# Narrower v pieces between the scores, weighted values in pairs, a first layer begun on two head pairs, two pieces swapped and one copy moved to ScalarE

## The chip, the cores and the metric

The kernel runs on one core of one Trainium2 chip. The metric is the time of one execution on the device, in microseconds (us). Each kernel was executed several times, in rounds in which the kernel before ran beside it on the same chip. Every execution counted here was fast (none was over 1.5% above the fastest of its kernel). Within that state the clock granted to TensorE (the share of its full rate that the profile shows as allowed) still differed from launch to launch (its mean over an execution was 0.968 to 0.978 in all runs but four, and 0.961 to 0.963 in those).

## The reference, cut to what matters

Attention over blocks of 96 tokens, with k and v mixed between blocks by a matrix P that five row and column normalisations make, then two dense layers with a squared Relu between.

```python
# q, k, v: 4 x 8 heads x 768 x 64; 8 blocks of 96 tokens; P: 4 x 8 x 8 x 8
k_sorted = np.einsum('bhij,bhjcd->bhicd', P, k_b)
v_sorted = np.einsum('bhij,bhjcd->bhicd', P, v_b)
...
attn = softmax(scale * q_b @ k_sb.T)      # inside each block
x    = (attn @ v_sb)                      # 3072 tokens x 512
h = x @ w_in                              # 512 x 2048
g = s * np.maximum(h, 0.0)**2 + b
out = g @ w_out                           # 2048 x 512
```

## The kernel before

Tokens are worked on in eight groups `t` of 384 (half of one batch's sequence). What concerns us is the start: the first group's attention, which has nothing else to run beside, and the first layer (`ffn1`) that follows it. Later groups' attention is cut into pieces that a queue puts between the matmuls of the layers.

```python
def warm_up(n, pool=psb):                 # dummy matmuls: 128 rows, 256 columns
    wp = pool.tile([128, 256], FP, ...)
    for _ in range(n):
        nc.tensor.matmul(out=wp, lhsT=zt[:, 0:128], rhs=zt, start=True, stop=True)

def v_piece0(d0, n, eng):                 # n of the 64 columns of sorted v
    # n > 8: a buffer of pool psa (3 of them); n <= 8: one of pool psb (2)
    ...                                   # n matmuls, one eviction on eng

def ffn1(t, slot=nothing, n0=0, nn=HB):   # first layer, 8 groups of 2 x 128 features
    for f0 in range(0, NF, 2):
        hps = psa.tile([128, 2, 512], FP, tag="a", name="hps")
        for f in range(2):
            for hp in range(NHP):         # 4 head pairs: 8 matmuls to a group
                nc.tensor.matmul(out=hps[:, f, 0:nt], lhsT=wi_at(hp, f0 + f), ...)
        rt = rtp.tile(...)
        nc.scalar.activation(out=rt, in_=hps, func=AF.Relu)          # ACT
        nc.vector.tensor_tensor(out=gt[...], in0=rt, in1=rt, op=ALU.mult)  # DVE
        slot()                            # a piece of other work
...
v_piece0(0, 16, "v")
v_piece0(16, 16, "s")
v_piece0(32, 16, "v")
s_piece(0, 0)                             # scores of a head pair, Exp on ACT
v_piece0(48, 8, "v")
s_piece(0, 1)
v_piece0(56, 8, "v")
s_piece(0, 2)
s_piece(0, 3)
for hp in range(NHP):
    p_piece(0, hp, 0, 2)                  # weighted values: 4 matmuls, then x on DVE
    if hp == 3:
        t_part(0, 0, "s", 0, 2)           # transposes of x, copy on ACT
    warm_up(2, psa)                       # two dummies after each: 8 here
t_part(0, 2, "v", 0, 2)
warm_up(2, psa)                           # and two more: 10 in all
```

In the profile, `tv` is a v piece, `sc` scores, `pv` weighted values, `x` their normalised form, `tr` transposes, `hps` the first layer, `rt` its Relu, `gt` the square, `ops` the second layer, `wp` a dummy. A dummy is a matmul whose result nobody reads; it is there to keep PE at work.

The softmax here doesn't subtract the row's maximum and nothing guards it: scores larger than these inputs give would overflow.

## Time and profile before

| what | value | where from |
|---|---|---|
| time | 233.06 us (233.01 to 233.14, 3 runs) | times |
| span of the profiled execution | 231.6 us | page |
| PE busy | 224.3 us, 97% | page, part 1 |
| DVE, ACT busy | 116.8 and 114.6 us, about 50% each | page, part 1 |
| clock at half rate | from 14.11 to 27.77 us | granted clock, read in ever narrower windows |
| first layer starts | 27.32 us | timeline |

PE, busy for 97% of the span, is the engine that bounds the kernel, so time leaves the total only where PE waits or runs at half clock.

### The profile page before, as it was taken

The numbers are of one execution on the slowest core, as the hardware profiler recorded it, in microseconds if no ns is written. First come the engines' busy times: TensorE is split into PE (matmuls) and PEld (weight loads), VectorE is DVE, ScalarE is ACT, GpSimd is POOL, SyncE is SP. The second block draws the span as 40 slices with busy tenths as digits, with TensorE's granted clock in tenths as the row PEclk, the third lists the DMA queues.
The fourth block names the chain that finished last, engine by engine and source line by source line (L and its number), as shares of the span: only waits on it lengthen the run. The fifth ranks groups of instructions, "written<-read, shape, count | busy, mean of one in ns | idle before, by whom it ended". The sixth has DMA issues, their size and how long they took to land.

```text
span 231.6 us, 4837 instructions
## 1 busy us (share of the span) xinstructions
PE 224.3 (97%) x2036; PEld 136.8 (59%) x2036; DVE 116.8 (50%) x245; ACT 114.6 (49%) x164; POOL 48.3 (21%) x62
## 2 busy tenths in 40 slices
PE   8879999999999999999999999999999999999994
PEld 6779887765544555566555555665555556554442
DVE  5778566638992645244446653343452634432221
ACT  6168479685158486856630645656222236660000
POOL 7820000399992000007920000000000000000000
PEclk9975699999999999999999999999999999999999
DMA  5999999998799992764999995610115240001212
GB/s 93 142 200 211 226 193 205 231 220 183 106 110 180 273 312 63 161 82 65 130 148 133 183 197 115 93 47 0 46 47 113 93 110 4 3 0 45 80 59 91
DMA packets 46695, 28.90 MB, mean 125 GB/s; under 512 B 35921, under 2 KB 41041, under 8 KB 46161
## 3 DMA queue, kind: packets, MB, share of 16 engines
q0 software_dynamic: 18800, 15.21, 47.8%
q1 hardware_dynamic: 27728, 13.32, 26.6%
q8 instruction: 16, 0.26, 0.5%
q10 hardware_dynamic: 144, 0.07, 0.1%
q14 instruction: 7, 0.05, 0.1%
HBM read 29.63 MB, written 8.65 MB: 165 GB/s over the span
## 4 chain that ended last, share of the span: by engine, by line
PE 82%; DVE 7%; DMA 5%; ACT 3%; issue 1%; POOL 0%; POOLq 0%
PE hps L473 35%; PE ops L516 31%; DMA qr<-in_q_dram 5%; PE pv L402 4%; PE sc L375 3%; DVE gt L478 2%; ACT ks L240 2%; DVE ks L238 2%; PE tv L320 2%; PE ops L501 2%; PE tk L294 1%; PE tv L350 1%; PE wp L182 1%; PE tq L254 1%; PE tv L336 1%
## 5 line engine op out<-in xcount | busy, mean ns | idle before, releaser
L473 PE MATMUL hps<-xt,wi 128*128 128x384 bf16 (+1 forms) x576 | 87.1, 309 | 0.3 <-ACT rt L477 0.3
L516 PE MATMUL ops<-wo,gt 128*128 128x512 bf16 x368 | 86.9, 380 | 0.4 <-DVE ot L490 0.4
L473 PEld LDWEIGHTS <-wi 128*128 128x128 bf16 x576 | 54.1, 98 | 30.6 <-issue 1.3
L477 ACT ACTIVATE rt<-hps 128x768 bf16<-128x768 f32 (+1 forms) x72 | 53.1, 741 | 37.4 <-PE hps L473 37.0
L478 DVE TENSOR_TENSOR gt<-rt 128x768 bf16<-128x768 bf16 (+1 forms) x72 | 41.2, 574 | 50.2 <-ACT rt L477 50.0
L516 PEld LDWEIGHTS <-gt 128*128 128x128 bf16 x368 | 33.6, 98 | 37.2 <-issue 1.0
L378 ACT ACTIVATE at<-sc 96x768 bf16<-96x768 f32 x32 | 24.4, 804 | 27.7 <-PE sc L375 27.7
L490 DVE SCALAR_TENSOR_TENSOR ot<-ops,s_bc,bias 128x512 f32<-128x512 f32 x23 | 17.1, 749 | 41.2 <-PE ops L516 41.2
L240 ACT CAST ks<-tk 64x512 bf16<-64x512 f32 (+1 forms) x32 | 18.6, 582 | 10.5 <-PE tk L294 10.2
L407 DVE TENSOR_TENSOR x<-pv,rec 96x512 bf16<-96x512 f32 (+1 forms) x36 | 22.6, 627 | 1.3
L639 POOL TENSOR_TENSOR csum<-csum,wo 128x512 f32<-128x512 f32 x14 | 17.6, 1254 | 1.0
L402 PEld LDWEIGHTS <-at 96*128 96x128 bf16 (+1 forms) x256 | 12.0, 104 | 3.8
L182 PE MATMUL wp<-zt 128*128 128x256 bf16 x86 | 12.9, 311 | 1.1 <-DVE warm L113 1.1
L238 DVE CAST ks<-tk 64x512 bf16<-64x512 f32 (+1 forms) x20 | 13.0, 651 | 1.1 <-PE tk L294 0.8
L402 PE MATMUL pv<-vs,at 96*128 96x66 bf16 (+1 forms) x256 | 13.0, 199 | 0.1
L240 ACT CAST vn<-tv 128x512 bf16<-128x512 f32 (+1 forms) x12 | 9.4, 799 | 7.2 <-PE tv L350 5.0
L375 PEld LDWEIGHTS <-ks 64*96 64x96 bf16 x256 | 8.6, 128 | 5.8 <-issue 5.1
L406 DVE RECIPROCAL rec<-pv 96x8 f32<-96x8 f32 (+1 forms) x36 | 6.9, 192 | 9.5 <-PE pv L402 9.4
L84 POOL DMA_DIRECT2D qr<-in_q_dram x12 | 10.6, 912 | 4.8 <-DMA kb<-in_k_dram 3.1
L375 PE MATMUL sc<-qt,ks 64*96 64x96 bf16 x256 | 10.9, 219 | 0.1
L182 PEld LDWEIGHTS <-zt 128*128 128x128 bf16 x86 | 9.0, 110 | 2.6 <-DVE warm L113 1.1
L294 PEld LDWEIGHTS <-kb 64*128 64x128 bf16 x192 | 6.7, 99 | 3.9 <-issue 3.4
(73 smaller groups left out, 98.4 us busy)
## 6 DMA issues: line engine op xcount, KB each, us to landing
out_dram<-ot SPq DMA_DIRECT2D x23, 256.0 KB, 2.4
kb<-in_k_dram POOLq DMA_DIRECT2D x4, 768.0 KB, 12.2
vb<-in_v_dram POOLq DMA_DIRECT2D x4, 768.0 KB, 19.0
wi<-in_moe_w_in_dram POOLq DMA_DIRECT2D x2, 1024.0 KB, 19.7
wo<-in_moe_w_out_dram POOLq DMA_DIRECT2D x2, 1024.0 KB, 32.6
qr<-in_q_dram POOLq DMA_DIRECT2D x12, 128.0 KB, 13.5
dv<-vn SPq DMA_DIRECT2D x6, 256.0 KB, 7.5
vs<-dv POOLq DMA_DIRECT2D x4, 384.0 KB, 12.7
```

The source lines that it names most:

```text
L182: nc.tensor.matmul(out=wp, lhsT=zt[:, 0:128], rhs=zt, start=True, stop=True)
L238: nc.vector.tensor_copy(out=out, in_=in_)
L240: nc.scalar.copy(out=out, in_=in_)
L375: nc.tensor.matmul(out=sc[:, e, n * BLK:(n + 1) * BLK], lhsT=ks[pr, g0 + n, :], rhs=QT[b][pr, hp, q0:q0 + BLK], start=True, stop=True)
L378: nc.scalar.activation(out=at, in_=sc[:, :, 0:TG], func=AF.Exp, scale=scale)
L402: nc.tensor.matmul(out=pv[e][0:m, (n - n0) * VW:(n - n0 + 1) * VW], lhsT=atf[:, c0:c0 + m], rhs=VS[b][:, gi, :], start=True, stop=True)
L407: nc.vector.tensor_tensor(out=x[:, n0:n0 + nn, hp * 128:(hp + 1) * 128].rearrange("p n (e d) -> p e n d", e=2), in0=pvv[:, :, :, 0:D], in1 ...
L473: nc.tensor.matmul(out=hps[:, f, 0:nt], lhsT=wi_at(hp, f0 + f), rhs=xt_at(t, hp, n0, nn), start=(hp == 0), stop=(hp == NHP - 1))
L477: nc.scalar.activation(out=rt[:, :, 0:nt], in_=hps[:, :, 0:nt], func=AF.Relu)
L478: nc.vector.tensor_tensor(out=gt[:, f0:f0 + 2, c0:c0 + nt], in0=rt[:, :, 0:nt], in1=rt[:, :, 0:nt], op=ALU.mult)
L516: nc.tensor.matmul(out=ops, lhsT=gt[:, f, m * 128:(m + 1) * 128], rhs=wo_at(f), start=(f == 0), stop=(f == NF - 1))
L639: nc.gpsimd.tensor_tensor(out=csum, in0=csum, in1=wo_at(f), op=ALU.add)
```

## The change

Its intent: in the stage ahead of the first layer, put a score piece after every 8-wide v piece, make two head pairs' weighted values share one buffer and one DVE product, and let the first layer begin two groups on the head pairs whose transposed x arrives first. Further on, it swaps a v piece with a weighted-values piece, and moves one copy of transposed q from DVE to ScalarE. I call these part 1, part 2 and part 3.

```diff
+    def p_pair(t, hp0, n0):                        # 8 matmuls, one buffer
+        p2 = psa.tile([128, 4, 256], FP, tag="a", name="pv")
...                                                 # one reciprocal, one product on DVE
-    def ffn1(t, slot=nothing, n0=0, nn=HB):
+    def ffn1(t, slot=nothing, n0=0, nn=HB, lead=0):
...
+        for f0 in range(0, lead, 2):
+            begun[f0] = psa.tile([128, 2, 512], FP, tag="a", name="hps")
+            products(f0, begun[f0], range(0, NHP // 2))
...
-    v_piece0(32, 16, "v")
-    s_piece(0, 0)
-    v_piece0(48, 8, "v")
-    s_piece(0, 1)
-    v_piece0(56, 8, "v")
-    s_piece(0, 2)
-    s_piece(0, 3)
     for hp in range(NHP):
-        p_piece(0, hp, 0, 2)
-        if hp == 3:
-            t_part(0, 0, "s", 0, 2)
-        warm_up(2, psa)
+        v_piece0(32 + 8 * hp, 8, "v")
+        s_piece(0, hp)
+    warm_up(2)
+    p_pair(0, 0, 0)
+    warm_up(2)
+    p_pair(0, 2, 0)
+    t_part(0, 0, "s", 0, 2)
+    warm_up(3)
     t_part(0, 2, "v", 0, 2)
-    warm_up(2, psa)
...
-                   ... SC(1, 0), SC(1, 1)], 8), 0, 2)
-    ffn1(0, Queue([..., V1(1), P(1, 2), P(1, 3),
+                   ... SC(1, 0), SC(1, 1)], 8), 0, 2, 4)
+    ffn1(0, Queue([..., P(1, 2), V1(1), P(1, 3),
...
-    qu = Queue([nothing, lambda: q_piece(1, 2, "v")]
+    qu = Queue([nothing, lambda: q_piece(1, 2, "s")]
```

More of the change, by code (lines that the diff above doesn't have):

```diff
@@ L410, in p_piece @@
             in1=rec[:, :, 0:nn].unsqueeze(3).broadcast_to([BLK, 2, nn, D]), op=ALU.mult)
+    def p_pair(t, hp0, n0):
+        b, half = divmod(t, 2)
+        if t not in X:
+            X[t] = xp.tile([BLK, HB, d_model], BF, tag="x", name="x")
+        p2 = psa.tile([128, 4, 256], FP, tag="a", name="pv")
+        for i in range(2):
+            atf = AT[t, hp0 + i].rearrange("p e t -> p (e t)")
+            for e in range(2):
+                for n in range(2):
+                    c0 = (e * HB + n0 + n) * BLK
+                    gi = e * 32 + (hp0 + i) * NB + half * HB + n0 + n
+                    nc.tensor.matmul(out=p2[:, 2 * i + e, n * VW:(n + 1) * VW],
+                                     lhsT=atf[:, c0:c0 + 128], rhs=VS[b][:, gi, :],
+                                     start=True, stop=True)
+        pvv = p2[0:BLK, :, 0:2 * VW].rearrange("p a (n w) -> p a n w", w=VW)
+        rec = rtp.tile([BLK, 4, 2], FP, tag="rec", name="rec2")
+        nc.vector.reciprocal(out=rec, in_=pvv[:, :, :, D])
+        nc.vector.tensor_tensor(
+            out=X[t][:, n0:n0 + 2, hp0 * 128:(hp0 + 2) * 128].rearrange(
+                "p n (a d) -> p a n d", d=D),
+            in0=pvv[:, :, :, 0:D], in1=rec.unsqueeze(3).broadcast_to([BLK, 4, 2, D]),
+            op=ALU.mult)
     def t_piece(t, eng, n0=0, nn=HB):
@@ L468, in ffn1, with products @@
         c0, nt = n0 * BLK, nn * BLK
-        for f0 in range(0, NF, 2):
-            hps = psa.tile([128, 2, 512], FP, tag="a", name="hps")
+        begun = {}
+        def products(f0, hps, part):
             for f in range(2):
-                for hp in range(NHP):
+                for hp in part:
                     nc.tensor.matmul(out=hps[:, f, 0:nt], lhsT=wi_at(hp, f0 + f),
@@ L475, in ffn1 @@
                                      start=(hp == 0), stop=(hp == NHP - 1))
+        for f0 in range(0, lead, 2):
+            begun[f0] = psa.tile([128, 2, 512], FP, tag="a", name="hps")
+            products(f0, begun[f0], range(0, NHP // 2))
+        for f0 in range(0, NF, 2):
+            if f0 in begun:
+                hps = begun[f0]
+                products(f0, hps, range(NHP // 2, NHP))
+            else:
+                hps = psa.tile([128, 2, 512], FP, tag="a", name="hps")
+                products(f0, hps, range(NHP))
             rt = rtp.tile([128, 2, TG], BF, tag="rt", name="rt")
@@ L621 @@
     ffn1(0, Queue([P(0, 0, 2, 2), P(0, 1, 2, 2), P(0, 2, 2, 2), P(0, 3, 2, 2),
-                   lambda: q_half(1, "s"), lambda: t_piece(0, "v", 2, 2), SC(1, 0), SC(1, 1)], 8), 0, 2)
-    ffn1(0, Queue([seq(SC(1, 2), P(1, 0)), V1(0), seq(SC(1, 3), P(1, 1)), V1(1), P(1, 2), P(1, 3),
+                   lambda: q_half(1, "s"), lambda: t_piece(0, "v", 2, 2), SC(1, 0), SC(1, 1)], 8), 0, 2, 4)
+    ffn1(0, Queue([seq(SC(1, 2), P(1, 0)), V1(0), seq(SC(1, 3), P(1, 1)), P(1, 2), V1(1), P(1, 3),
                    seq(V1(2), V1(3)), lambda: t_piece(1, "v")], 8), 2, 2)
```

## The prediction

> **What bounds the kernel now.** I read the page first, then the busy time and granted clock by window, then the timeline and the chain of waits in the three places that the change touches.
>
> ```profile
> PE   8879999999999999999999999999999999999994
> PEclk9975699999999999999999999999999999999999
> ...
> PE 82%; DVE 7%; DMA 5%; ACT 3%; issue 1%; POOL 0%; POOLq 0%
> ```
> TensorE is busy nearly everywhere and is 82% of the chain that ended last. From about 70 us on the chain lists almost only PE pieces, so a microsecond taken out before that should come out of the total. But slices 2 to 4 ran at a reduced clock. The windows[...]:
>
> ```profile
> 17.52:20.93 3.41, 3.27 (x41) 3.22 (x41) 2.60 (x4) 3.10 (x6) 0.00 (x0) 0.50 1.13 211
> 20.93:24.35 3.42, 3.32 (x55) 3.14 (x54) 2.69 (x5) 2.63 (x4) 0.53 (x1) 0.50 1.12 213
> 24.35:27.75 3.40, 3.40 (x32) 2.76 (x31) 2.56 (x8) 0.97 (x2) 0.00 (x0) 0.50 1.16 226
> 27.75:31.17 3.42, 3.42 (x51) 3.22 (x50) 2.15 (x9) 1.75 (x4) 0.00 (x0) 1.00 1.03 198
> ```
> Columns: busy PE, weight loads, DVE, ACT, POOL, then the clock. The clock is 0.50 until 27.75 us, so the stage that the change rebuilds (v pieces, scores, first weighted values, 16.2 to 27.3 us) runs wholly at half rate. PE is covered, yet two dependences matter there:
>
> ```profile
> 14.86 4.80 ACT L240 CAST ks<-tk 64x512 bf16<-64x512 f32 x8
> ...
> 22.97 0.69 DVE L238 CAST vs<-tv 96x512 bf16<-96x512 f32 x1 [0.20 <-PE tv L320]
> ...
> 27.32 1.05 PE L473 MATMUL hps<-xt,wi 128*128 128x192 bf16 x8
> ```
> ACT's eight key evictions end at 19.66. The last v eviction (22.97 to 23.66) releases the first weighted values. The first layer starts at 27.32. Later, in the chain of waits:
>
> ```profile
> 41.75 0.68 PE hps L473 x8
> 42.42 0.02 issue
> 42.45 0.50 ACT rt L477
> 42.95 0.04 issue
> 42.99 0.82 PE hps L473 x8
> ```
> PE waits for a Relu that frees a PSUM buffer, about 0.47 us.
>
> ```profile
> 57.19 4.29 DVE gt L478 x3
> 61.48 1.67 DVE qt L238
> 63.15 0.59 DVE ks L238
> ...
> 68.73 0.76 DVE bias L561
> 69.52 0.76 DVE ot L490
> 70.28 0.04 issue
> 70.32 1.02 PE ops L516 x4
> ```
> DVE is a chain without a gap from 57 to 70.3 us, and PE waits at its end.
>
> [...] half rate lasts from 14.11 to 27.75 us, four times 3.41. So time saved before 27.75 is worth half[...]. [...] the 128x768 squares take 557 ns at 49.4 us and 1507 ns by 57.1 us, while GpSimd sums w_out; this is why DVE is late, and the change leaves it alone.
>
> **Part 1: the stage to the first layer.** The same 64 v and 32 score matmuls remain; the v pieces become 16, 16, 8, 8, 8, 8, with a score piece after each 8. I took each wait from the order of instructions and the semaphores of the changed program, and each duration from the trace.
> - Before, the third v piece (16) takes a buffer that is free and starts at 19.36 without a wait. After, the first 8-piece takes the small buffer whose ACT evictions end at 19.66: start 19.71, a new wait of 0.35.
> - At half rate an 8-piece costs 0.70 and a score piece 0.31 (8 v plus 8 scores: 21.07 to 22.08). Four pairs from 19.71 end at 23.73 (before: 23.37).
> - The last 8-piece ends on PE about 23.6 (23.43 plus its latency); its DVE eviction (0.69) ends at 24.33 (before 23.66). The two dummy matmuls fit in the gap. First pair of weighted values: 24.38 to 24.83 on PE, results 25.03.
> - DVE per pair: reciprocal 0.20 + product 0.69 = 0.92 with the issue, against 2 x 0.65 = 1.30 for two single ones (0.18 + 0.42 and gaps). First pair's x at 25.98; second pair's results at 25.94, x at 26.92.
> - First transposes 26.04 to 26.36; three dummies (0.21 each) to 27.0; second transposes 27.0 to 27.32. ACT's copy of the first half is done at 27.12. So the first layer starts at 27.32, by chance the same as before.
> - Beginning two groups on head pairs 0 and 1 puts 8 matmuls ahead of the copy on DVE (done 27.99). Before, two dummies (0.42) did that. Dummies go from 10 to 7, but the time goes into the wait for v and into DVE.
> Sum: 0.0, give or take 0.3, since what is gained or lost runs at half rate. A gain beyond 0.38 would meet the second half of w_in, which landed at 30.42 and is first read at 30.80.
>
> **Part 2: value piece swapped.** Now: group 3 of the second half at 39.56, v piece 40.31, group 4 40.64, values 41.31, group 5 41.58, values 42.25, group 6 42.99. The last step takes 0.74 where the same step earlier takes 0.27: 0.47 of wait. Changed: group 3 39.56, values 40.23, group 4 ready at 40.50 but its buffer is freed by the DVE product that ends at 40.74, so 40.79 (new wait 0.28); v piece 41.54, group 5 41.87, values 42.54, group 6 42.81; its buffer was free by 42.13. Gain 0.47 - 0.28 = 0.18.
>
> **Part 3: q copy on ScalarE.** ACT is idle from 58.97 to 63.75. ACT took 1.44 for the same copy at 47.19; from 60.65 it ends at 62.1, before ACT's next piece at 63.75: free. DVE loses 1.67. The key matmuls of 61.54 release their results at 62.18, so DVE then does four evictions of 0.69 to 65.0, four more to 68.07 (results there from 65.26), bias to 68.85 (was 69.48), output row to 69.64 (was 70.27). PE: from the start of the scores at 69.18 to the next w_out group took 1.13 us; the same step at 72.57 took 0.49. The excess, 0.64, is two waits: the second score piece for bias (0.14 or more) and the group for the row. Afterwards the group could start at 69.67 and is released at 69.69. Gain 0.62.
>
> Total: 0.0 - 0.18 - 0.62 = -0.80 us, all ahead of the PE-bound stretch: 233.06 - 0.80 = 232.26.
>
> **Rivals.**
> - The clock comes back one window later (31.17), because three dummies are gone and PE waits 0.3 for x: then 3.41 us at half rate cost about 1.7, giving 234.0. For: window 24.35 to 27.75 falls from 3.40 busy to about 3.0 (estimate from the starts above). Against: the first rise, three windows before 14.11 at 3.87, followed a window in which PE had worked only from 1.13 on, 2.74 of 3.41, with the same dummies. About 8%.
> - It comes back one window earlier, at 24.35, because scores are packed with v: about 0.6 better, 231.6. Against: that window keeps about the same matmuls and had not sufficed. About 5%.
> - Part 1 gains what its author hoped: if the 0.35 wait or the late v eviction is hidden better than I think, 0.2 to 0.3 more, 232.0.
> - The gain is absorbed: GpSimd's sum of w_out ends at 64.96 whatever PE does (its start follows the last x at 44.3); the bias matmul needs it, at 66.06 before. The slack of 1.1 holds against 0.2 of shift. Value reads of batch 1 landed at 71.07 and are needed at 76.3. If DVE stays late anyway (squares slower still), part 3 gives only part of 0.62: 232.6.
>
> **Range and chances.** Parts 2 and 3 rest on waits measured to some 0.1; part 1 is worth 0.3 either way; the clock adds a tail on both sides. Range 231.7 to 233.1. No route reaches 2% (4.7 us): even a clock two windows off is less. Faster 0.01, same 0.98, slower 0.01.
>
> **What would show it.** Right: half rate still ends at 27.75; the first 8-wide v piece starts at 19.7, after ACT; the first layer starts near 27.3; no Relu wait of 0.5 near 42.5 but a DVE wait of 0.3 near 40.6; no PE wait for the output row near 70, and the w_out group that began at 70.32 begins about 69.5. Wrong: a first layer start off by more than 0.3, a clock record moved by a window, or PE still waiting for DVE at 69 to 70 us.

The sum: 0.0 - 0.18 - 0.62 = -0.80 us, that is 232.26 us. To read with it:

- A "window" there and below is a stretch of 3.41 us, counted from a change of the clock. The measure comes from these profiles: full rate held for 10.24 us (3 x 3.41) from 3.87 to 14.11 us, half rate for 13.65 (4 x 3.41) to 27.77. The rise at 3.87 shows in the dummies, which start 0.21 us apart before it and 0.11 after (the clock column has no record from before 3.87 and prints 1.00 there). What the two rivals on the clock give as reasons (dummies, waits, packing) were conjectures when they were written.
- "Worth half" is an estimate from the granted clock of 0.50 up to 27.75. The pair's times on DVE (0.20 and 0.69) are estimates from the same shapes later in this trace: a reciprocal of 96x8 took 197 ns and a product of 96x512 took 686 ns on average. The "latency" is 0.2 us: the last v piece starts at 22.08, its matmuls account for 0.70, and its eviction starts at 22.97.
- GpSimd's sums of w_out run from 44.73 to 64.96 us, beside the short square and the long ones alike. That they are what slows the squares was not shown.

## The result, and the profile after

The changed kernel took 233.84 us (median of 4 runs, 233.58 to 233.99). The kernel before took 233.10 us in the same rounds (4 runs, 233.01 to 233.14). The ratio is 1.0031, with a 95% interval from 1.0014 to 1.0049. Ratios here and below are the mean time of one kernel's fast runs over the mean of the other's in the same rounds, so they are not quite the ratio of the medians quoted. In these rounds the change made the kernel a little slower. I had expected 0.80 us less, and 233.1 at the most.

The two profiles, by their landmarks (us from the start of the span):

| landmark | before | after | after minus before |
|---|---|---|---|
| first weighted values on PE | 23.71 | 24.41 | +0.70 |
| first layer starts | 27.32 | 27.31 | -0.01 |
| clock is full again | 27.77 | 29.48 | +1.71 |
| q transposes inside the first layer | 31.60 | 32.67 | +1.07 |
| first layer of t=1 starts | 47.08 | 48.10 | +1.02 |
| w_out group after the bias | 70.32 | 70.75 | +0.43 |
| span | 231.6 | 232.2 | +0.6 |

The stage itself came out as worked out. The whole loss arises between the first layer's start and the q transposes, some 5 us; part 2 gives back 0.05 and part 3 gives back 0.59.

The page of the changed kernel, with busy PE and the granted clock:

```profile
PE   8979999999999999999999999999999999999994
PEclk9985599999999999999999999999999999999998
```

Each digit is a fortieth of the span (5.8 us). PE is filled as before. The clock row is different: the reduced slices have moved to the right.

The windows of the changed kernel, with edges 3.41 us apart, counted back from the clock's return at 29.48 us (the columns are start and end, length, busy PE, PE weight loads, DVE, ACT and POOL with their counts, then the granted clock, the DMA share and GB/s):

```profile
22.65:26.07 3.42, 3.27 (x43) 2.53 (x41) 2.34 (x5) 1.79 (x3) 0.53 (x1) 0.50 1.13 215
26.07:29.48 3.41, 3.41 (x27) 2.98 (x28) 1.11 (x3) 0.49 (x2) 0.00 (x0) 0.50 1.16 228
```

Half rate lasted from 15.82 to 29.48 us, 13.65 us, as long as before (14.11 to 27.77), but 1.71 us later. So 2.17 us of the first layer ran at half rate in this launch; before, only 0.45 us did.

The timeline of the rebuilt stage of the changed kernel (start, length, engine, line, operation, in brackets the idle time before it and what ended that):

```profile
19.79 0.66 PE L320 MATMUL tv<-pd,vb 64*128 64x64 bf16 x6 [0.20 <-ACT ks L240]
...
23.66 0.69 DVE L238 CAST vs<-tv 96x512 bf16<-96x512 f32 x1 [0.31 <-PE tv L320]
...
24.41 0.62 PE L424 MATMUL pv<-vs,at 96*128 96x66 bf16 x8
...
26.05 0.50 PE L467 MATMUL tr<-ident,x 96*128 96x96 bf16 x4 [0.15 <-DVE x L430]
```

The first 8-wide v piece waits for ACT, as the prediction had it (19.71 expected, 19.79 seen). The last v eviction ends at 24.35 (24.33 expected), the first pair starts at 24.41 (24.38), and the transposes wait for DVE's x at 26.05 (26.04).

The timeline of the start of the first layer, changed kernel:

```profile
27.31 2.12 PE L498 MATMUL hps<-xt,wi 128*128 128x192 bf16 x12
...
29.47 1.04 ACT L513 ACTIVATE rt<-hps 128x384 bf16<-128x384 f32 x2 [2.40 <-PE hps L498]
...
30.95 0.31 PE L402 MATMUL pv<-vs,at 96*128 96x66 bf16 x4 [0.17 <-DVE x L407]
```

and the first Relu of the kernel before:

```profile
28.40 0.49 ACT L477 ACTIVATE rt<-hps 128x384 bf16<-128x384 f32 x1 [1.53 <-PE hps L473]
```

Two things are to be seen. Twelve matmuls of the first layer took 2.12 us, at half rate. And since two groups were begun together, they also end together: ACT meets two Relus in a row (x2, 1.04 us), the first over a microsecond later than before. DVE gets its work in a lump, and PE then waits 0.17 us for an x that DVE makes after it.

The chain of the changed kernel at the swapped pieces (start, length, what):

```profile
40.61 0.36 DVE gt L514
...
41.11 0.70 DVE x L407
...
41.86 0.83 PE hps L498 x8
```

and its timeline where the first layer of t=1 starts:

```profile
48.10 6.29 PEld L498 LDWEIGHTS <-wi 128*128 128x128 bf16 x40 [0.20 <-DVE xt L238]
```

PE's wait for a Relu is gone, and one for DVE's product has come, as expected: from the values at 41.32 to the group at 41.86 it is 0.54 us, where the step without a wait took 0.27 (41.31 to 41.58 before), so 0.27 of wait where 0.28 was expected. What I had not followed further is the line of the timeline: the later pieces meet DVE again, whose copy of the transposed x releases the next layer 0.20 us late.

The timeline at the q copy and at the output rows, changed kernel:

```profile
61.70 1.44 ACT L240 COPY qt<-tq 128x1536 bf16<-128x1536 bf16 x1 [1.71 <-PE tq L269]
...
69.95 1.41 DVE L526 SCALAR_TENSOR_TENSOR ot<-ops,s_bc,bias 128x512 f32<-128x512 f32 x2
...
70.75 1.02 PE L552 MATMUL ops<-wo,gt 128*128 128x512 bf16 x4
```

ACT was idle for 1.71 us before the copy and took 1.44 for it, as assumed. PE's group at 70.75 now starts with no wait in front of it. From the bias matmul to that group it takes 3.67 us (67.08 to 70.75), where it took 4.26 before (66.06 to 70.32).

### The profile page after: what moved, and what is told of

It is laid out like the page before. It is cut to its first block, busy times and chain, and to the rows that moved or that the text cites. A ratio compares the mean times of both kernels' runs of the same rounds, so it can differ in the third digit from the quotient of the medians.

```text
span 232.2 us, 4807 instructions
## 1 busy us (share of the span) xinstructions
PE 223.8 (96%) x2013; PEld 136.7 (59%) x2033; DVE 115.3 (50%) x241; ACT 116.1 (50%) x165; POOL 48.2 (21%) x62
## 4 chain that ended last, share of the span: by engine, by line
PE 87%; ACT 5%; DVE 5%; issue 1%; DMA 1%
PE hps L498 36%; PE ops L552 34%; PE sc L375 4%; PE pv L402 3%; ACT ks L240 3%; PE tk L294 2%; PE ops L537 2%; PE tv L350 1%; PE tv L320 1%; PE tq L254 1%; PE tv L336 1%; DMA sn<-in_sort_net_dram 1%; PE tq L269 1%; ACT qt L240 1%; DVE rstat L203 1%
## 5 line engine op out<-in xcount | busy, mean ns | idle before, releaser
L552 PE MATMUL ops<-wo,gt 128*128 128x512 bf16 x349 | 83.8, 379 | 1.2 <-issue 0.3
L407 DVE TENSOR_TENSOR x<-pv,rec 96x512 bf16<-96x512 f32 (+1 forms) x32 | 20.9, 653 | 1.2
L402 PEld LDWEIGHTS <-at 96*128 96x128 bf16 x240 | 10.7, 103 | 3.7 <-issue 0.5
L402 PE MATMUL pv<-vs,at 96*128 96x66 bf16 x240 | 11.5, 196 | 0.2 <-DVE x L407 0.2
L375 PE MATMUL sc<-qt,ks 64*96 64x96 bf16 x256 | 11.4, 219 | 0.1
L406 DVE RECIPROCAL rec<-pv 96x8 f32<-96x8 f32 (+1 forms) x32 | 6.2, 194 | 9.0 <-PE pv L402 9.0
L294 PEld LDWEIGHTS <-kb 64*128 64x128 bf16 x192 | 6.2, 95 | 3.9 <-issue 3.0
```

The costliest lines, as they stand in the source:

```text
L375: nc.tensor.matmul(out=sc[:, e, n * BLK:(n + 1) * BLK], lhsT=ks[pr, g0 + n, :], rhs=QT[b][pr, hp, q0:q0 + BLK], start=True, stop=True)
L402: nc.tensor.matmul(out=pv[e][0:m, (n - n0) * VW:(n - n0 + 1) * VW], lhsT=atf[:, c0:c0 + m], rhs=VS[b][:, gi, :], start=True, stop=True)
L407: nc.vector.tensor_tensor(out=x[:, n0:n0 + nn, hp * 128:(hp + 1) * 128].rearrange("p n (e d) -> p e n d", e=2), in0=pvv[:, :, :, 0:D], in1 ...
L552: nc.tensor.matmul(out=ops, lhsT=gt[:, f, m * 128:(m + 1) * 128], rhs=wo_at(f), start=(f == 0), stop=(f == NF - 1))
```

## The experiments

My theory after the result: half rate falls at another place in each launch, and with three dummies fewer and the waits for v and for x, the rebuilt stage gets its clock back only at the end of a later window. The rivals: the begun groups cost the time (bunching); parts 2 or 3 cost it somewhere late; or the two profiles merely differ in where half rate fell, by chance.

A word on the clock counts below. In the profiles half rate always lasts a whole number of windows of 3.41 us: 10.24, 13.65 or 17.07 us are three, four or five. An unprofiled run shows it through its mean clock: 0.976 to 0.978 goes with three, 0.968 to 0.971 with four, 0.961 to 0.963 with five. (A second drop just before the end of some runs, at 230.87 us in the changed kernel's profile, makes the spread inside each.) "3 of 6" below means that three of six runs had three windows.

| label | median us (range, runs) | before, same rounds | ratio (95%) | runs with three windows |
|---|---|---|---|---|
| e1_before_again | 233.52 (233.19 to 233.96, 4) | 233.39 | 1.0007 (0.9990 to 1.0024) | 2 of 4 |
| e1_after_again | 233.84 (232.99 to 234.00, 4) | 233.39 | 1.0012 (0.9990 to 1.0033) | 0 of 4 |
| e1_part1 | 234.53 (234.25 to 234.95, 4) | 233.39 | 1.0055 (1.0038 to 1.0072) | 0 of 4 |
| e1_parts23 | 232.63 (232.51 to 233.33, 4) | 233.39 | 0.9974 (0.9954 to 0.9993) | 2 of 4 |
| e2_dense | 233.35 (233.09 to 233.75, 6) | 233.41 | 0.9997 (0.9984 to 1.0010) | 3 of 6 |
| e2_few | 233.73 (233.20 to 234.17, 6) | 233.41 | 1.0013 (0.9998 to 1.0029) | 0 of 6 |
| e2_order | 234.97 (233.82 to 235.63, 6) | 233.41 | 1.0061 (1.0039 to 1.0084) | 0 of 6 |
| e2_pairs | 233.83 (233.46 to 234.33, 6) | 233.41 | 1.0019 (1.0004 to 1.0035) | 1 of 6 |
| e3_lead_only | 233.67 (233.23 to 234.24, 6) | 233.69 | 1.0004 (0.9985 to 1.0023) | 3 of 6 |
| e3_lead2 | 233.46 (233.05 to 233.94, 6) | 233.69 | 0.9994 (0.9975 to 1.0012) | 1 of 6 |
| e3_best | 233.30 (232.68 to 235.72, 6) | 233.69 | 0.9999 (0.9960 to 1.0039) | 2 of 6 |
| e3_parts23_again | 233.26 (232.67 to 233.40, 6) | 233.69 | 0.9978 (0.9959 to 0.9996) | 1 of 6 |
| e4_half_rows | 235.70 (235.55 to 236.19, 6) | 233.47 | 1.0093 (1.0078 to 1.0109) | 0 of 6 |
| e4_plus | 233.39 (233.07 to 233.89, 6) | 233.47 | 0.9992 (0.9977 to 1.0007) | 1 of 6 |

All outputs are right. The kernel before itself had three windows in 4 of 7, 5 of 11, 2 of 11 and 6 of 11 runs in the four sets of rounds, 17 of 40.

### e1_before_again and e1_after_again: both kernels once more

Edit: none. These two only show how much a launch decides.

> The kernel before, unchanged, as a control. Theory A ([...]where the half-rate stretch falls is a matter of the launch): its profile may show the drop and the return at other times than 14.11 and 27.75 us, still 13.65 us apart, and the time moves by up to about 1 us with it. Theory B (the changed stage itself delays the clock): drop at 14.1 and return at 27.75 again, 233.1 us.

> The changed kernel, unchanged, as a control. Theory A: drop and return at another offset than 15.83 and 29.48 us; with a return near 27.7 the time is near 232.4 us, with 29.5 near 233.8. Theory B: again a return near 29.5 and 233.8 us.

The windows ahead of the clock's return, in the kernel before:

```profile
20.27:23.69 3.42, 3.42 (x57) 3.33 (x56) 2.57 (x4) 2.41 (x4) 0.35 (x1) 0.50 1.13 214
23.69:27.10 3.41, 3.30 (x34) 2.69 (x34) 2.48 (x9) 1.73 (x3) 0.18 (x1) 0.50 1.19 229
```

and in the changed kernel:

```profile
23.44:26.85 3.41, 3.26 (x38) 2.35 (x35) 2.37 (x5) 1.45 (x3) 0.53 (x1) 0.50 1.18 225
26.85:30.26 3.41, 3.41 (x28) 3.17 (x27) 0.64 (x3) 0.74 (x2) 0.00 (x0) 0.50 1.00 208
```

In this launch of the kernel before, half rate ran from 16.86 to 27.10 us, three windows; in the first it had run from 14.11 to 27.77, four. So half rate did not stand at a fixed place of the program. The changed kernel had 16.61 to 30.26. Most telling: the window 20.27 to 23.69 had PE busy for all of its 3.42 us and half rate went on after it, while 23.69 to 27.10 had 3.30 and the clock was back at its end. In the changed kernel half rate went on after 3.26. Busy time does not tell these windows apart.

The time of the changed kernel against before was not separated in this set (1.0012, an interval across 1). By the means of the same rounds the loss was 0.73 us in the first set and 0.28 in this one, 0.5 on average. In the first set all four runs of before lay within 0.13 us, at the low end of what it does elsewhere (233.01 to 234.40 in 44 runs), so that comparison may show the loss somewhat large.

### e1_part1 and e1_parts23: the change taken apart

e1_part1 is the changed kernel with parts 2 and 3 undone; e1_parts23 is the kernel before with parts 2 and 3 done:

```diff
-    ... seq(SC(1, 3), P(1, 1)), V1(1), P(1, 2), P(1, 3),
+    ... seq(SC(1, 3), P(1, 1)), P(1, 2), V1(1), P(1, 3),
...
-    qu = Queue([nothing, lambda: q_piece(1, 2, "v")]
+    qu = Queue([nothing, lambda: q_piece(1, 2, "s")]
```

> Only the stage before the first layer changed (v pieces, pairs, begun groups, 7 dummies), not the swap and not the q copy. From my step sums it starts the first layer at 27.3 us like before. Theory A: 233.1 us when the clock returns near 27.7, up to 234 when it returns near 29.5, so it scatters with the clock record. Theory B: about 234.5 us (233.8 plus the 0.7 of the two other parts), always with the late return.

> Only the value piece swapped and the q copy on ScalarE, the stage before the first layer as before. Both theories: part 2 gives about 0.15 and part 3 about 0.6, so 0.75 us less than the kernel before at the same place of the clock record, 232.3 us. Theory A allows 0.9 more if the clock returns later; theory B says 232.3 with a return at 27.75.

Part 1 alone is slower, by 0.0055 x 233.39 = 1.3 us, and no run of it had three windows. Parts 2 and 3 alone are faster, by 0.0026 x 233.39 = 0.6 us. This removes the rival that parts 2 or 3 cost the time: all of the loss is in part 1. In the profile of part 1 half rate ended at 28.70 us and the q transposes came at 32.38; in that of parts 2 and 3 it ended at 26.54 and they came at 31.49. The last half-rate window of part 1, with 3.26 us of busy PE, is one at whose end the clock was back:

```profile
25.29:28.70 3.41, 3.26 (x29) 2.77 (x28) 1.88 (x4) 0.48 (x1) 0.00 (x0) 0.50 1.18 235
```

### e2_dense and e2_few: only the dummies

e2_dense gives the changed kernel its three dummies back, where PE waited for x; e2_few takes three from the kernel before.

```diff
# e2_dense, against the changed kernel
     p_pair(0, 2, 0)
+    warm_up(3)
     t_part(0, 0, "s", 0, 2)
# e2_few, against the kernel before
-        warm_up(2, psa)
+        warm_up(1 if hp < 3 else 2, psa)
```

> The changed kernel with three more dummy matmuls after the second pair of weighted values, where PE idled 0.34 us: 10 dummies as before. First layer about 27.6 us instead of 27.3. If the share of a window in which PE streams decides when the clock returns (density), some executions come with three half-rate windows (mean clock 0.978) as in the kernel before, and the median falls to about 233.0 in spite of the 0.3 later start. If only the chance place of the windows counts, it stays at four windows (0.971 or less) always and comes out at 233.8 plus 0.15 = 234.0.

> The kernel before with three dummy matmuls taken out of the first weighted values (7 as in the changed kernel), all else as before. PE then reaches the first layer up to 0.6 us earlier, at half rate. Density: executions with three half-rate windows become rarer or vanish, and the time is the same as before or up to 0.5 worse. Chance alone: the shares of 0.978 and 0.971 stay, and the time falls by 0.3 us.

With ten dummies the changed kernel had three windows in 3 of 6 runs, where with seven it had them in 0 of 8. The kernel before with seven had them in 0 of 6, and with ten, beside it, in 5 of 11. Each comparison is small, but both edits touch the dummies alone and point the same way; the changed kernel, e1_part1 and e2_few together have 0 of 18, the kernel before 17 of 40, or 19 of 44 with e1_before_again. So the dummies mattered for the clock here. Their number is not all: below, e2_order has 0 of 6 with ten of them, and e2_pairs and e3_best have 1 of 6 and 2 of 6 with seven. In time, e2_dense no longer differs from before (0.9997), although it carries the gains of parts 2 and 3 and keeps PE busy for all of the 3.41 us from 24.61 to 28.02, across the first layer's start; the step of begun groups still cost it something, as e3_lead_only shows. e2_few is slower than before by 0.3 us, with an interval that touches 1.

### e2_order and e2_pairs: the halves of part 1

e2_order is the kernel before with only the new order of v and score pieces (ten dummies). e2_pairs is the kernel before with the pairs, the begun groups and the seven dummies, in the old order.

```diff
# e2_order, against the kernel before
-    v_piece0(32, 16, "v")
-    s_piece(0, 0)
...
+    for hp in range(NHP):
+        v_piece0(32 + 8 * hp, 8, "v")
+        s_piece(0, hp)
# e2_pairs, against the kernel before
-    for hp in range(NHP):
-        p_piece(0, hp, 0, 2)
...
+    warm_up(2)
+    p_pair(0, 0, 0)
+    warm_up(2)
+    p_pair(0, 2, 0)
+    t_part(0, 0, "s", 0, 2)
+    warm_up(3)
...                              # and lead=4 in the first ffn1
```

> The kernel before with only the order of scores and smaller v pieces changed; single weighted values and all 10 dummies kept. By my steps the first weighted values start 0.67 us later (24.4 for 23.7), PE idles there, and the first layer starts near 28.0 instead of 27.3: 233.7 to 234.1, so this part alone loses 0.3 to 0.7.

> The kernel before with only the pairs, the 7 dummies and the begun groups; scores and v pieces in the old order. By my steps the first layer starts near 26.8 instead of 27.3, worth 0.3 us at half rate: 233.1 if the clock is not touched; under density, with fewer dummies, the return comes later and eats it: 233.4 to 233.9.

The new order alone is the worst single step of the change: 1.0061, or 1.4 us, where I had expected 0.3 to 0.7. PE stands idle for 0.42 us, until 24.42, for the last v eviction, since here no dummies stand ahead of the first weighted values, the first layer starts at 28.02 instead of 27.32, and no run had three windows, with ten dummies as before. So the narrower pieces gain nothing: the first of them waits for ACT and the last eviction comes 0.7 us later. The pairs alone bring the first layer forward to 26.95 and still lose (1.0019), with the clock back only at 28.47 in the profile: an earlier layer at half rate, with fewer dummies ahead of it.

### e3_lead_only and e3_lead2: the begun groups

e3_lead_only is the kernel before with two groups begun. e3_lead2 is e2_dense with one group begun instead of two.

```diff
# e3_lead_only, against the kernel before
-  ... SC(1, 0), SC(1, 1)], 8), 0, 2)
+  ... SC(1, 0), SC(1, 1)], 8), 0, 2, 4)
# e3_lead2, against e2_dense
-  ... SC(1, 0), SC(1, 1)], 8), 0, 2, 4)
+  ... SC(1, 0), SC(1, 1)], 8), 0, 2, 2)
```

> The kernel before with only this: the first two groups of the first layer are begun on head pairs 0 and 1. Theory C (bunching): both Relus then come close together, the third pair of weighted values finds its buffer still in use and waits about 0.3 us for DVE, so the stretch from the first layer's start to the second q turn grows from 4.28 to about 4.6 us, and the time from 233.4 to 233.7. If the begun groups are harmless, 4.28 us and 233.4.

> The changed kernel with 10 dummies, and one group begun instead of two. Theory C: no wait for the product of the first weighted values near 30.4 us, about 0.3 us less than with two groups: 233.05 against 233.35. If two groups are no harm: 233.35.

The profile of e3_lead_only had its clock back at 27.09, before the layer, so the begun groups stand there without the clock's part. Its timeline:

```profile
29.93 0.31 PE L402 MATMUL pv<-vs,at 96*128 96x66 bf16 x4 [0.25 <-DVE x L407]
```

PE waits 0.25 us for DVE's x. From the layer's start to the q transposes it takes 4.39 us, against 4.28 before: the begun groups cost 0.11. With one group begun (e3_lead2) that step takes 4.38, against 4.65 in e2_dense, but the two aren't clean to compare: e2_dense had 0.53 us of the layer at half rate in its profile and e3_lead2 0.14, which accounts for some 0.2 of the 0.27 (an estimate: half of 0.53 - 0.14, by the granted clock of 0.50). The layer also starts 0.17 later, and in time the two can't be told apart (0.9994 and 0.9997): my expectation of a clear gain was a miss. The bunching is real and small, and as the main cause of the loss it falls.

### e3_best and e3_parts23_again: a version that beats both?

e3_best joins what seemed good: the old order, pairs, dummies 3, 1 and 3, one begun group, parts 2 and 3. e3_parts23_again repeats parts 2 and 3 alone, unchanged.

```diff
# e3_best, against the kernel before (the rest as in e2_pairs, and parts 2 and 3)
+    p_pair(0, 0, 0)
+    warm_up(3)
+    p_pair(0, 2, 0)
+    warm_up(1)
+    t_part(0, 0, "s", 0, 2)
+    warm_up(3)
```

> Scores and v pieces in the old order, pairs of weighted values at once after the last score, 7 dummies placed where PE would idle (3, 1, 3), one group begun, the swap and the q copy on ScalarE. First layer near 26.9 us instead of 27.3. If only idle gaps count for the clock, some executions have three half-rate windows and the time is 232.3, 0.2 under the version with parts 2 and 3 alone; if the dummies count as such (7 against 10), four windows nearly always, and 232.6 to 233.2.

> The kernel before with only the swap and the q copy moved, once more beside the others: 232.6 us, 0.7 to 0.8 under the kernel before of the same rounds, with both three and four half-rate windows among its executions.

e3_best starts its first layer at 26.73 us, the earliest of all, and settles nothing: 0.9999 with a wide interval, one run of six at 235.72. Parts 2 and 3 alone were faster again, 0.9978 with an interval below 1. Two sets agree, so the version that beats both kernels is the kernel before with parts 2 and 3 only, by 0.5 to 0.6 us.

### e4_half_rows and e4_plus: do the dummies' rows count, and can one add dummies?

Still open was what sets apart the windows at whose end the clock was back. e4_half_rows lets the ten dummies use 64 rows of the array instead of 128, with the same columns. e4_plus adds two dummies to e1_parts23 ahead of the first weighted values, where PE waits for v.

```diff
# e4_half_rows, against the kernel before
-            nc.tensor.matmul(out=wp, lhsT=zt[:, 0:128], rhs=zt, start=True, stop=True)
+            nc.tensor.matmul(out=wp, lhsT=zt[0:r, 0:128], rhs=zt[0:r], ...)   # r = 64
# e4_plus, against e1_parts23
     s_piece(0, 3)
+    warm_up(2)
     for hp in range(NHP):
```

> The kernel before, but its 10 dummies before the first layer use 64 of the 128 rows of the array: same columns, same number, same gaps. If a window is judged by streamed columns weighted with the rows in use (the weighting that separates all 14 profiles: 0.73 and less never brought the clock back, 0.81 and more always did), the earliest window end that suffices moves from 25.8 to about 28.3 us: no execution with three half-rate windows, first layer start unchanged near 27.3, mean time about 234.5. If only the time that PE is busy or streams counts, rows not: a third to a half of the executions at 0.978 and 233.4.

> The version with only the swap and the q copy moved, and two full dummies more, in the 0.34 us in which PE waits for the last v eviction before the first weighted values. First layer about 0.1 us later than without them. By the weighting, the earliest sufficient window end moves from 25.8 to about 25.3 us: more executions with three half-rate windows (two thirds instead of a third), mean 0.1 to 0.2 under the 233.0 of that version. If the weighting is wrong: 233.05, a third.

With 64 rows the kernel became slower by 0.0093 x 233.47 = 2.2 us (235.7 us, where I had expected 234.5), and four of six runs had five windows, which nothing else had. A window of it, and the two lines of its timeline at the first weighted values:

```profile
24.62:28.04 3.42, 3.42 (x27) 1.67 (x26) 2.06 (x7) 0.81 (x2) 0.00 (x0) 0.50 1.18 232
```

```profile
24.14 0.60 PE L183 MATMUL wp<-zt 64*128 64x256 bf16 x2
24.68 0.24 PEld L403 LDWEIGHTS <-at 96*128 96x128 bf16 x4 [0.41 <-issue]
```

The window was busy from edge to edge (3.42 of 3.42 us) and half rate still went on after it. But the test is not clean: next to a 64-row dummy the weight load stood 0.41 us at issue, so the dummies also spread out and the first layer started at 28.59, not near 27.3 as I had expected. That rows count is supported by this run, not settled.

e4_plus was a miss. The dummies started at 23.92, when v was nearly ready (its last eviction ended at 24.05), and the first weighted values came at 24.59, 0.5 us after it, and the layer at 28.20. Without the two dummies, in e1_parts23, they came 0.04 us after the eviction (23.84). It has three windows in 1 of 6, and its 0.9992 is no gain on the 0.9974 and 0.9978 without them, though the intervals overlap. Here the dummies ran past the wait that they were to fill and held up work that was ready.

### What sorted these windows

I added up, for each window of the 16 profiles at half rate, what PE streamed: per matmul its columns over 1.2 per ns, times the used rows over 128. The 1.2 is read from the traces: at half rate two dummies of 256 columns take 0.63 us and three take 0.84, so one more takes 0.21 = 256/1.2. Example, the last half-rate window of the kernel before, 24.35 to 27.77: 12 weighted values of 66 columns on 96 rows, 8 dummies of 256 on 128, 8 transposes of 96 on 96 and 3 of the first layer of 192 on 128. That is 594 + 2048 + 576 + 576 = 3794 columns, over 1.2 it is 3.16 us, 0.93 of 3.41; with the matmuls at the edges cut, 0.91. (Score and v matmuls use 64 rows: the profile lists them as 64*96 and 64*128.)

| kernel, window | PE busy | streamed share | clock back at its end |
|---|---|---|---|
| e1_before_again 20.27 to 23.69 | 3.42 | 0.55 | no |
| changed kernel 22.65 to 26.07 | 3.27 | 0.62 | no |
| before 20.93 to 24.35 | 3.32 | 0.64 | no |
| e1_after_again 23.44 to 26.85 | 3.26 | 0.72 | no |
| e2_pairs 21.64 to 25.05 | 3.41 | 0.73 | no |
| e1_parts23 23.13 to 26.54 | 3.31 | 0.81 | yes |
| e1_part1 25.29 to 28.70 | 3.26 | 0.83 | yes |
| e1_before_again 23.69 to 27.10 | 3.30 | 0.86 | yes |
| before 24.35 to 27.77 | 3.40 | 0.91 | yes |
| changed kernel 26.07 to 29.48 | 3.41 | 0.94 | yes |

Over all 16 profiles, with the first rise after the start, no window with 0.73 or less had the clock back at its end and every one with 0.81 or more had. Below, the first are said to have failed and the second to have sufficed. Busy PE does not sort them: 3.42 failed and 3.26 sufficed. It is a description of these windows, worked out afterwards, and one other measure sorts them as well: weighted by the used columns of the array too, 0.70 and less failed and 0.78 and more sufficed. Streamed columns without any weight do not sort them (1.12 failed, 0.81 sufficed), nor does the weighted share without the transposes of x (0.73 failed, 0.68 sufficed). The drops fit it too. At full rate a matmul streams 2.4 columns per ns (four of 512 take 0.86 us, from 70.32 to 71.18 in the kernel before); so counted, the window ahead of the first drop had 0.22 to 0.38 in each profile, and every other full-rate window that ended before 226 us had 0.60 or more and kept the rate. In the kernel before it is this window, with 0.31; PE was never idle in it for more than 1.04 us at a stretch (0.34 to 1.30 us over the 16 profiles):

```profile
10.69:14.11 3.42, 2.26 (x79) 1.88 (x77) 1.73 (x9) 0.64 (x1) 1.38 (x2) 1.00 1.15 231
```

That the chip itself weighs columns and rows is not shown by this.

Taking the middle, 0.77, as the mark, I estimated from each profile's matmuls when a window that suffices could end at the earliest: at 25.8 to 25.9 us in the kernel before and in e1_parts23, at 27.3 in the changed kernel and e1_part1. The rebuilt stage moves it by 1.5 us, from well before the first layer to its very start. That fits the counts. In the 16 profiles the drop came between 14.11 and 16.86 us, so three windows after it end between 24.35 and 27.10: a stage that suffices from 25.8 on is caught in some launches, one that suffices from 27.3 on in none. The earliest end is 27.3 for e2_order with ten dummies (0 of 6) and 26.0 for e3_best with seven (2 of 6). So by this measure what counted here is when the dense stretch comes, and dummies are one way to make it dense.

## Why the prediction was right or wrong

**Part 1, its sum of 0.0: the layer's start was right, the step behind it failed.** Each start that I worked out was met within 0.1 us, down to the first layer at 27.31. The step that failed is "time saved before 27.75 is worth half", and with it "half rate still ends at 27.75" and the 8% given to the rival. I took 27.75 as a property of the program, which the change leaves alone or moves by a whole window; this was an assumption of mine, and in the profiled pair the return moved by 1.71 us, half a window. It is one launch's: the kernel before had its clock back at 27.77 and at 27.10 in two profiles, and at 26.54 and 28.59 in two of the same stage with parts 2 and 3. So the rebuilt stage does not add a window to every launch, as the rival had it; it takes the early return from the launches that had it (19 of 44 runs before, 0 of 8 after). The rival's reasons, fewer dummies and PE's wait for x, were part of the cause, as e2_dense, with three dummies in that wait, and e2_few show (3 of 6 runs with three windows against 0 of 8, and 0 of 6 against 5 of 11). By the measure above the program sets from when on a window suffices, and the launch sets where the windows fall: the drop came at 14.11 and at 16.86 us in two profiles of the kernel before. Nor does busy PE sort the windows, so my "3.40 busy to about 3.0" measured the wrong thing, and so did my argument against the rival (the window before 3.87, busy for 2.74 us, streamed 0.81): from 24.35 to 27.75 us busy fell only from 3.40 to 3.25 and the streamed share from 0.91 to 0.78.

The size: three profiles of the rebuilt stage (changed kernel twice, e1_part1) reach the q transposes at 32.67, 32.77 and 32.38 us, mean 32.61; four of the old stage (before twice, parts 2 and 3 twice) at 31.60, 31.55, 31.49 and 32.03, mean 31.67. Part 1 costs 0.94 us by that landmark, on a handful of launches. The 1.3 us of e1_part1's times, with an interval from 0.9 to 1.7, don't contradict it.

**Beginning two groups**, which I had put down as a mere exchange of dummies for first-layer work, costs 0.11 us by itself: both groups end together, and DVE's x comes late (e3_lead_only). In the profiled launch the step from the layer's start to the q transposes grew by 1.08 us, from 4.28 to 5.36. With the same begun groups and no half rate in the layer it took 4.39 (e3_lead_only), so 0.11 is the begun groups and 0.97 the half rate. The profiles with begun groups grow with it: 4.65 with 0.53 us of the layer at half rate (e2_dense), 5.06 with 1.38 (e1_part1), 5.36 with 2.17. The 0.45 us at half rate in the kernel before cost nothing: e1_before_again and e1_parts23 had none and took 4.28 as well.

**Part 2, 0.18 expected:** the Relu wait went and the product wait came at the right size. At the q transposes of the next turn 0.15 is still there (14.68 us from 31.60 to 46.28 before, 14.53 from 32.67 to 47.20 after). But at the next layer only 0.05 is left (15.48 us from 31.60 to the first layer of t=1 before, 15.43 after), and the same in e1_parts23 (15.43). The sum stopped too early: four groups later DVE is late again, by the 0.20 seen at 48.10. The record shows where: DVE's product ahead of that copy of x took 0.53 or 0.54 us in four profiles with part 2 and 0.36 or 0.37 in three without, and in all seven it ended 0.21 to 0.23 us after the first of GpSimd's sums of w_out. The swap brought it onto that sum; that this is why it took longer, no run tested.

**Part 3, 0.62 expected:** right. 0.59 in the profiled pair, 0.59 to 0.61 over all profiles with it.

**The total.** 0.94 - 0.05 - 0.60 gives +0.29 us. The two sets of rounds showed 0.73 and 0.28. (The means over all runs differ by 233.74 - 233.48 = 0.26, but that sets rounds in which the changed kernel did not run against those in which it did.) That the change is slower rests on the first set and on e1_part1 against e1_parts23; its size is known to a few tenths only.

**What stays open.** Whether rows alone or rows and columns of the array are the better weight for sorting the windows, and where between 0.73 and 0.81 the mark lies, if it is one: e4_half_rows was not clean. Why the stretch from the w_out group near 70 us to the end scatters from 161.2 to 162.1 us between profiles, of unchanged code too (161.25 and 161.53 in the two of the kernel before); that is as large as what is measured here. And no run set where half rate falls in a launch, so that was not tried directly.

## What to carry to other kernels

Where the clock record changes inside a stage, do not take the time at which it came back in one profile as the program's own: here it was 27.77 and 27.10 us in two profiles of one kernel. Ask which 3.4 us of the program it could follow; what PE streamed in them sorted the windows here (0.73 and less failed, 0.81 and more sufficed), and how busy it looked did not (3.42 us failed, 3.26 sufficed). Taking three dummies out had a price here (none of 6 runs with three windows, against 5 of 11). Compare several launches and their clock records before believing a few tenths. And run the parts of a change apart: here two small edits gained 0.5 to 0.6 us and the large rebuilding lost more than that.
